# SwiGLU feed-forward: one weight load and ten half-width matmuls change places with a crossbar copy and the gate matmuls behind it

## The chip, the cores and the metric

The kernel runs on one core of a Trainium2 chip. The metric is the device time of one execution in microseconds. Before the change the median of three runs is 163.51 us (163.34 to 163.87).

## What is computed

```python
B, S, D, F = 1, 2048, 640, 1536       # bfloat16, seeded normal values
def reference(x, w_gate, w_up, w_down):
    g = silu(x @ w_gate)              # [2048, 1536]
    u = x @ w_up                      # [2048, 1536]
    return (g * u) @ w_down           # [2048, 640]
```

## The kernel before

The 2048 rows of x are cut into four blocks of 512. D = 640 is five slices of 128 (`KD`), F = 1536 is twelve chunks of 128 (`KF`, "f chunk"). For each block and each f chunk TensorE computes gate (into a PSUM tile `pg`) and up (into `pu`), each as five accumulating matmuls over the slices of D, with the weights stationary and x, turned so that D lies on the partitions (`xT`), streaming through in up to 512 columns. ScalarE then writes `sg`, the Silu of `pg`, to SBUF, and VectorE multiplies it by `pu` into `aT`. After the twelve chunks of a block come the matmuls with `w_down` (`po_t`, `po_a`), their copies out and the stores. Beside all this VectorE computes the last four rows' gate and up as dot products (`do_dots`), from weights that crossbar copies turn (`wgT`, `wuT`).

The change is in `head()`, the first block's first four chunks (`EARLY = 4`), and in the order of the loads ahead of it. x comes in two ways. Rows 0-255 are loaded as they are (`x_sb`), turned on TensorE against an identity, and copied out of PSUM by ScalarE and VectorE. Rows 256-511 are turned on the way in, by a crossbar copy (`turn_x(HALF, S_BLK)`, a `dma_start_transpose`). In the trace this copy is the `DMA_TRANSPOSE` of line 105, the plain weight loads are line 83 (`load_w`) and line 115 (the early gate weights, one slice of D at a time), and every gate or up matmul is line 193 (`proj_step`).

`head()` runs 18 warm-up matmuls on a tile of ones, the turning of rows 0-255, then gate of all four chunks on rows 0-255 (slice by slice, the four chunks in turn, in the order in which the slices of `w_gate` arrive; slice 0 in two pieces of 128 rows), then gate of the four chunks on rows 256-511, and then, chunk by chunk, up on all 512 rows and the Silu and multiply (`gate()`).

```python
        steps = [(0, 0, P), (0, P, HALF)]
        steps += [(kd, 0, HALF) for kd in range(1, KD)]
        steps += [(kd, HALF, S_BLK) for kd in range(KD)]
```

Orders are written out by hand: `keep_order` pins the instructions of TensorE, ScalarE, VectorE and SyncE to the order of the program text. Nearly all loads are issued by SyncE, so its issue order is the order in which they enter its DMA queue: x rows 0-127, four slices of the early gate weights (ScalarE issues x rows 128-255 and one more slice), the crossbar copy of rows 256-511, up of chunks 0-1, up of chunks 2-3, gate and up of chunks 4-7, gate and up of chunks 8-11, `w_down`, the crossbar copy of rows 512-1023, and the inputs of the dot products.

The eight PSUM banks are four for `pg` and `pu` (tag `gu`) and two each under the tags `po_a` and `po_b`; the turning of rows 0-255 and the first four `pu` tiles use the latter four.

Of the kernel before, what the change touches and what calls it, by code (L numbers as in the profile page):

```python
# [10 lines left out]
def _body(  # L11
# [8 lines left out]
    nc = tc.nc  # L20
    P = nc.NUM_PARTITIONS
    f32 = mybir.dt.float32
# [10 lines left out]
    KD = D // P  # L33
    KF = F // P
    S_BLK = 512
    NSB = S // S_BLK
    SUB = S_BLK // P
    HALF = S_BLK // 2
# [4 lines left out]
    WT_STEP = 4  # L43
    ROW_J = 0
    EARLY = 4
    W_CHUNKS = [(4, 8), (8, 12)]
    assert D % P == 0 and F % P == 0 and S % S_BLK == 0 and D > DA and SUB == 4

# [3 lines left out]
    psum = ctx.enter_context(  # L52
        tc.tile_pool(name="psum", bufs=2, space=bass.MemoryType.PSUM)
    )
# [4 lines left out]
    wg_sb = consts.tile([P, KD, F], bf16)  # L59
    wu_sb = consts.tile([P, KD, F], bf16)  # L60
# [15 lines left out]
    wu_v = w_up.rearrange("(kd p) f -> p kd f", p=P)  # L76
    wd_v = w_down.rearrange("(kf p) d -> p kf d", p=P)

    def wslice(a, b):
        return slice(a * P, b * P)  # L80

    def load_w(eng, dst, src, a, b):
        eng.dma_start(out=dst[:, :, wslice(a, b)], in_=src[:, :, wslice(a, b)])
# [14 lines left out]
    def keep_order(engine):  # L98

        traced = [i for i in nc.cur_bb.bb.instructions if i.engine == engine]  # L100
        for a, b in zip(traced, traced[1:]):
            issue_order(a, b)

    def turn_x(r0, r1):
        nc.sync.dma_start_transpose(out=xT[:, :, r0:r1], in_=xt_v[r0:r1])
# [7 lines left out]
    for kd in range(KD):  # L113
        eng = nc.scalar if kd == 1 else nc.sync
        eng.dma_start(
            out=wg_sb[:, kd, wslice(0, EARLY)], in_=wg_v[:, kd, wslice(0, EARLY)]
        )
    turn_x(HALF, S_BLK)
    nc.scalar.activation(silu_first[:], ones[:, 0:1], ACT.Silu)  # L119
    for a in range(0, EARLY, 2):  # L120
        load_w(nc.sync, wu_sb, wu_v, a, a + 2)
    for a, b in W_CHUNKS:
        load_w(nc.sync, wg_sb, wg_v, a, b)
        load_w(nc.sync, wu_sb, wu_v, a, b)
# [49 lines left out]
    def warm(n):  # L174
        for _ in range(n):
            nc.tensor.matmul(  # L176
                pw[:, 0:P], lhsT=ones[:], rhs=ones[:], start=True, stop=True
            )

    def transpose_chunk(c, parts):  # L180
        c_sl = slice(c * P, (c + 1) * P)
        for copy, tag, k0, k1 in parts:
            pt = psum.tile([P, k1 - k0, P], bf16, tag=tag, name="pt")
            for kd in range(k0, k1):
                nc.tensor.transpose(  # L185
                    out=pt[:, kd - k0, :],
                    in_=x_sb[:, c, kd * P : (kd + 1) * P],
                    identity=ident[:],
                )
            copy(out=xT[:, k0:k1, c_sl], in_=pt[:])  # L190

    def proj_step(ps, w_sb, fc, sb, c0, c1, kd):
        nc.tensor.matmul(  # L193
            ps[:, c0:c1],
            lhsT=w_sb[:, kd, fc * P : (fc + 1) * P],
            rhs=xT[:, kd, sb * S_BLK + c0 : sb * S_BLK + c1],
            start=(kd == 0 and c0 in (0, HALF)),
            stop=(kd == KD - 1),
        )

    def proj(ps, w_sb, fc, sb, c0, c1):
        for kd in range(KD):
            proj_step(ps, w_sb, fc, sb, c0, c1, kd)

    def gu_tiles():
        pg = psum.tile([P, S_BLK], f32, tag="gu", name="pg", bufs=4)
        pu = psum.tile([P, S_BLK], f32, tag="gu", name="pu", bufs=4)
        return pg, pu

    def gate(pg, pu, sb, fc, n_s):  # L210

        s0 = sb * S_BLK
        sg = work.tile([P, S_BLK], f32, name="sg")
        nc.scalar.activation(sg[:, 0:n_s], pg[:, 0:n_s], ACT.Silu)  # L214
        nc.vector.tensor_tensor(  # L215
            out=aT[:, fc, s0 : s0 + n_s], in0=sg[:, 0:n_s], in1=pu[:, 0:n_s], op=ALU.mult
        )

    def head():
        dve, act = nc.vector.tensor_copy, nc.scalar.copy  # L220
        split = [(act, "po_a", 0, 2), (dve, "po_b", 2, KD)]
        pgs = [
            psum.tile([P, S_BLK], f32, tag="gu", name="pg", bufs=4)
            for _ in range(EARLY)
        ]
        warm(N_WARM)
        for c in range(HALF // P):
            transpose_chunk(c, split)

        steps = [(0, 0, P), (0, P, HALF)]  # L230
        steps += [(kd, 0, HALF) for kd in range(1, KD)]
        steps += [(kd, HALF, S_BLK) for kd in range(KD)]
        for kd, c0, c1 in steps:
            for fc in range(EARLY):
                proj_step(pgs[fc], wg_sb, fc, 0, c0, c1, kd)

        for fc in range(EARLY):
            pu = psum.tile([P, S_BLK], f32, tag=("po_a", "po_b")[fc % 2], name="pu")
            proj(pu, wu_sb, fc, 0, 0, S_BLK)
            gate(pgs[fc], pu, 0, fc, S_BLK)  # L240
        keep_order(mybir.EngineType.PE)
        keep_order(mybir.EngineType.Activation)

    head()
    for sb in range(NSB):
        n_s = S_BLK if sb < NSB - 1 else S_BLK - T
        for fc in range(KF):
            if sb == 0 and fc < EARLY:
                continue
            pg, pu = gu_tiles()  # L250
# [135 lines left out]
def kernel(tc, *args):  # L386
    _body(tc, *args)
    tc.close()
    tc.compile()
    _trim(tc.nc)  # L390
# [30 lines left out]
```

## Time and profile before

| | before |
|---|---|
| median time | 163.51 us |
| lowest, highest of 3 runs | 163.34, 163.87 us |
| span of the profiled execution, first to last instruction | 161.8 us |
| TensorE busy | 159.4 us (99% of the span) |
| VectorE busy | 111.0 us (69%) |
| ScalarE busy | 42.6 us (26%) |
| HBM read, written | 6.88 MB, 2.62 MB |

The profile was taken in an execution of its own; the page gives its span, and no time with launch and end for it, so that its 161.8 us are set beside the times of the other runs. In the views "PE" is TensorE's matmuls, "PEld" its weight loads, "ACT" ScalarE, "DVE" VectorE, "SPq" and "ACTq" the DMA issues of SyncE and ScalarE. A timeline row gives the start in us, the length from the first of the merged instructions to the end of the last, the engine and line, what is written from what, and the count; the idle time ahead of it and what ended that stand in brackets. A matmul's length includes its passage through the array, so the pace of a stream of matmuls is read from their starts and counts, not from one length. "DMA to landing" is the time from the start of a DMA's issue to the last signal of its data.

### The profile page before, as it was taken

How to read it: one execution, taken by the hardware profiler on the slowest of the kernel's cores; microseconds unless marked ns; L12 is line 12 of the kernel's file. 1: busy time of each engine (PE TensorE's matmuls, PEld its weight loads, DVE VectorE, ACT ScalarE, POOL GpSimd, SP SyncE). 2: the span in 40 equal slices, each digit the busy share in tenths (PEclk: the TensorE clock that was granted, in tenths of full speed). 3: DMA queues.
4: the chain of work that ended last, by engine and by line, in shares of the span. 5: the costliest groups of instructions: out<-in, count | busy, mean ns of one | idle time of the engine just before them, and what ended most of it. 6: DMA issues, size and time to landing. Idle time of an engine off the chain costs nothing.

```text
span 161.8 us, 2142 instructions
## 1 busy us (share of the span) xinstructions
PE 159.4 (99%) x808; PEld 77.6 (48%) x808; DVE 111.0 (69%) x250; ACT 42.6 (26%) x74; POOL 0.6 (0%) x6
## 2 busy tenths in 40 slices
PE   8999999999999999999999999999999999999995
PEld 7854444444444444444444444444444444445454
DVE  2034223599569999989919999979964999993001
ACT  5051222112222222211222322221214222222121
POOL 1000000000000000000000000000000000000000
PEclk9999999999999999999999999999999999999999
DMA  6999999934189999003110000000321000000312
GB/s 212 231 351 349 361 248 231 222 75 91 34 192 159 235 236 184 4 0 34 65 65 0 0 4 2 0 0 3 62 67 34 0 0 0 0 0 4 48 41 73
DMA packets 41961, 15.86 MB, mean 98 GB/s; under 512 B 33504, under 2 KB 41824, under 8 KB 41952
## 3 DMA queue, kind: packets, MB, share of 16 engines
q1 hardware_dynamic: 33584, 14.93, 37.0%
q10 hardware_dynamic: 8368, 0.80, 3.5%
q8 instruction: 6, 0.10, 0.3%
q14 instruction: 3, 0.02, 0.1%
HBM read 6.88 MB, written 2.62 MB: 59 GB/s over the span
## 4 chain that ended last, share of the span: by engine, by line
PE 97%; DMA 2%; SPq 0%; DVE 0%; issue 0%
PE pg L193 32%; PE pu L193 32%; PE po_a L291 26%; PE po_t L261 6%; DMA wg_sb<-in_w_gate_dram 2%; SPq L86 0%; DVE ot_b L302 0%
## 5 line engine op out<-in xcount | busy, mean ns | idle before, releaser
L193 PE MATMUL pg<-xT,wg_sb 128*128 128x512 bf16 (+3 forms) x264 | 59.8, 363 | 0.1
L193 PE MATMUL pu<-xT,wu_sb 128*128 128x512 bf16 (+1 forms) x240 | 59.1, 379 | 0.0
L215 DVE TENSOR_TENSOR aT<-sg,pu 128x512 bf16<-128x512 f32 (+1 forms) x48 | 32.7, 682 | 32.3 <-PE pu L193 32.3
L214 ACT ACTIVATE sg<-pg 128x512 f32<-128x512 f32 (+1 forms) x48 | 28.4, 597 | 71.2 <-PE pg L193 67.4
L291 PE MATMUL po_a<-wd_sb,aT 128*128 128x512 bf16 (+4 forms) x228 | 42.8, 348 | 0.0
L147 DVE SCALAR_TENSOR_TENSOR prod<-wgT,x_row 128x640 f32<-128x640 bf16 x48 | 39.4, 821 | 1.5 <-DMA wgT<-in_w_gate_dram 0.4
L147 DVE SCALAR_TENSOR_TENSOR prod<-wuT,x_row 128x640 f32<-128x640 bf16 x48 | 39.4, 821 | 1.0
L193 PEld LDWEIGHTS <-wg_sb 128*128 128x128 bf16 x264 | 25.9, 100 | 26.8 <-DMA wg_sb<-in_w_gate_dram 0.4
L193 PEld LDWEIGHTS <-wu_sb 128*128 128x128 bf16 x240 | 23.4, 98 | 28.1 <-DMA wu_sb<-in_w_up_dram 0.3
L291 PEld LDWEIGHTS <-aT 128*128 128x128 bf16 x228 | 20.8, 98 | 21.7
L300 ACT CAST ot<-po_a 128x512 bf16<-128x512 f32 (+2 forms) x17 | 9.5, 559 | 31.8 <-PE po_a L291 20.2
L261 PE MATMUL po_t<-aT,wd_sb 128*128 128x512 bf16 (+1 forms) x48 | 10.4, 366 | 0.0
L261 PEld LDWEIGHTS <-wd_sb 128*128 128x128 bf16 x48 | 4.7, 98 | 5.1
L302 DVE CAST ot_b<-po_a 128x96 bf16<-128x96 f32 (+1 forms) x2 | 0.5, 240 | 9.7 <-PE po_a L291 9.6
L270 ACT CAST ot_t<-po_t 128x512 bf16<-128x512 f32 (+1 forms) x4 | 2.2, 559 | 11.6 <-PE po_t L261 11.6
L147 DVE DVE_READ_ACCUMULATOR prod<-wgT,x_row 128x1 f32 x48 | 3.9, 82 | 0.0
L147 DVE DVE_READ_ACCUMULATOR prod<-wuT,x_row 128x1 f32 x48 | 3.9, 82 | 0.0
L272 DVE STREAM_TRANSPOSE ot_q<-ot_t 128x512 bf16<-128x512 bf16 (+1 forms) x4 | 2.7, 676 | 1.7 <-ACT ot_t L270 1.7
L190 DVE COPY xT<-pt 128x384 bf16<-128x384 bf16 x2 | 0.7, 358 | 2.9 <-PE pt L185 2.9
L176 PE MATMUL pw<-ones 128*128 128x128 bf16 x18 | 2.1, 313 | 0.4 <-DVE ones L109 0.4
L176 PEld LDWEIGHTS <-ones 128*128 128x128 bf16 x18 | 1.8, 147 | 0.4 <-DVE ones L109 0.4
L119 ACT ACT_TABLE_LOAD x1 | 1.3, 1283 | 1.0 <-issue 1.0
(13 smaller groups left out, 4.7 us busy)
## 6 DMA issues: line engine op xcount, KB each, us to landing
wd_sb<-in_w_down_dram SPq DMA_DIRECT2D x1, 1920.0 KB, 13.0
out_dram<-ot SPq DMA_DIRECT2D x15, 128.0 KB, 1.7
wg_sb<-in_w_gate_dram SPq DMA_DIRECT2D x2, 640.0 KB, 7.9
wu_sb<-in_w_up_dram SPq DMA_DIRECT2D x2, 640.0 KB, 8.6
wu_sb<-in_w_up_dram SPq DMA_DIRECT2D x2, 320.0 KB, 4.7
x_row<-in_x_dram SPq DMA_DIRECT2D x1, 640.0 KB, 5.1
wg_sb<-in_w_gate_dram SPq DMA_DIRECT2D x4, 128.0 KB, 3.4
out_dram<-ot_q ACTq DMA_DIRECT2D x12, 32.0 KB, 1.9
```

Of the source, the lines that this page charges most:

```text
L119: nc.scalar.activation(silu_first[:], ones[:, 0:1], ACT.Silu)
L147: nc.vector.scalar_tensor_tensor(out=prod[:], in0=wT[:, fc, :], scalar=1.0, in1=x_row[:, t, :], op0=ALU.mult, op1=ALU.mult, accum_out=acc[ ...
L176: nc.tensor.matmul(pw[:, 0:P], lhsT=ones[:], rhs=ones[:], start=True, stop=True)
L190: copy(out=xT[:, k0:k1, c_sl], in_=pt[:])
L193: nc.tensor.matmul(ps[:, c0:c1], lhsT=w_sb[:, kd, fc * P : (fc + 1) * P], rhs=xT[:, kd, sb * S_BLK + c0 : sb * S_BLK + c1], start=(kd == 0 ...
L214: nc.scalar.activation(sg[:, 0:n_s], pg[:, 0:n_s], ACT.Silu)
L215: nc.vector.tensor_tensor(out=aT[:, fc, s0 : s0 + n_s], in0=sg[:, 0:n_s], in1=pu[:, 0:n_s], op=ALU.mult)
L261: nc.tensor.matmul(po_t[:], lhsT=wd_sb[:, kf, DA:D], rhs=aT[:, kf, sb * S_BLK : sb * S_BLK + n_t], start=(kf == 0), stop=(kf == KF - 1),)
L270: nc.scalar.copy(ot_t[:], po_t[:])
L272: nc.vector.transpose(out=ot_q[:], in_=ot_t[:])
L291: nc.tensor.matmul(po[:], lhsT=aT[:, kf, s0 : s0 + P], rhs=wd_sb[:, kf, c0:c1], start=(kf == 0), stop=(kf == KF - 1),)
L300: nc.scalar.copy(ot[:], po[:])
```

## The change

The up weights of chunks 0 and 1 (`UP_FIRST = 2`, 320 KB) are loaded ahead of the crossbar copy of rows 256-511 instead of behind it. On TensorE, up of chunks 0 and 1 on rows 0-255 (ten matmuls of 256 columns) runs between gate on rows 0-255 and gate on rows 256-511. Later, up of these two chunks runs on rows 256-511 alone (ten matmuls of 256 columns), in place of ten matmuls of 512 columns. The four `pu` tiles of `head()` are allocated together ahead of the loops. TensorE has ten matmuls and ten weight loads more in all.

```diff
+    UP_FIRST = 2
...
+    load_w(nc.sync, wu_sb, wu_v, 0, UP_FIRST)
     turn_x(HALF, S_BLK)
     nc.scalar.activation(silu_first[:], ones[:, 0:1], ACT.Silu)
-    for a in range(0, EARLY, 2):
-        load_w(nc.sync, wu_sb, wu_v, a, a + 2)
+    load_w(nc.sync, wu_sb, wu_v, UP_FIRST, EARLY)
...
         steps = [(0, 0, P), (0, P, HALF)]
         steps += [(kd, 0, HALF) for kd in range(1, KD)]
-        steps += [(kd, HALF, S_BLK) for kd in range(KD)]
         for kd, c0, c1 in steps:
             for fc in range(EARLY):
                 proj_step(pgs[fc], wg_sb, fc, 0, c0, c1, kd)
 
+        pus = [
+            psum.tile([P, S_BLK], f32, tag=("po_a", "po_b")[fc % 2], name="pu")
+            for fc in range(EARLY)
+        ]
+        for fc in range(UP_FIRST):
+            proj(pus[fc], wu_sb, fc, 0, 0, HALF)
+        for kd in range(KD):
+            for fc in range(EARLY):
+                proj_step(pgs[fc], wg_sb, fc, 0, HALF, S_BLK, kd)
         for fc in range(EARLY):
-            pu = psum.tile([P, S_BLK], f32, tag=("po_a", "po_b")[fc % 2], name="pu")
-            proj(pu, wu_sb, fc, 0, 0, S_BLK)
-            gate(pgs[fc], pu, 0, fc, S_BLK)
+            proj(pus[fc], wu_sb, fc, 0, HALF if fc < UP_FIRST else 0, S_BLK)
+            gate(pgs[fc], pus[fc], 0, fc, S_BLK)
```

## The prediction

> **What bounds the kernel now.** I read the page first, then the chain of waits in order of time, then the timeline of the first 15 us, and last the single transfers of that stretch.
>
> ```profile
> span 161.8 us, 2142 instructions
> PE 159.4 (99%) x808; PEld 77.6 (48%) x808; DVE 111.0 (69%) x250; ACT 42.6 (26%) x74; POOL 0.6 (0%) x6
> PE 97%; DMA 2%; SPq 0%; DVE 0%; issue 0%
> ```
>
> ```profile
> 0.45 3.21 DMA wg_sb<-in_w_gate_dram
> 3.71 5.21 PE pg L193 x44
> 8.92 4.37 PE pu L193 x20
> 13.29 1.08 PE pg L193 x5
> ...
> 148.85 11.10 PE po_a L291 x84
> ```
>
> TensorE carries 97% of the chain. From 13.29 on every piece of the chain is TensorE's, five matmuls of 512 columns in 1.08 us (0.216 each), one piece behind the other until the last at 148.85. So the span is the time at which TensorE is through its first four chunks, plus a constant. What the change can win or lose lies between 3.71 and about 14, and a microsecond there is a microsecond of the result.
>
> ```profile
> 0.13 0.38 ACTq L86 DMA_DIRECT2D x_sb<-in_x_dram  x1
> 0.45 1.84 SPq L115 DMA_DIRECT2D wg_sb<-in_w_gate_dram  x4
> 2.33 1.91 SPq L105 DMA_TRANSPOSE xT<-in_x_dram  x1
> 4.29 1.15 SPq L83 DMA_DIRECT2D wu_sb<-in_w_up_dram  x2
> 6.06 0.92 SPq L83 DMA_DIRECT2D wu_sb<-in_w_up_dram  x1
> 8.79 4.00 PEld L193 LDWEIGHTS <-wu_sb 128*128 128x128 bf16 x20 [0.15 <-DMA wu_sb<-in_w_up_dram]
> 8.79 4.49 PE L193 MATMUL pu<-xT,wu_sb 128*128 128x512 bf16 x20
> 14.06 0.89 PEld L193 LDWEIGHTS <-wu_sb 128*128 128x128 bf16 x5 [0.19 <-DMA wu_sb<-in_w_up_dram]
> 14.20 1.24 PE L193 MATMUL pu<-xT,wu_sb 128*128 128x512 bf16 x5
> ```
>
> The same timeline, asked for TensorE alone in two narrow windows, shows the place where rows 256-511 are awaited:
>
> ```profile
> 6.27 0.57 PE L193 MATMUL pg<-xT,wg_sb 128*128 128x256 bf16 x3
> 6.57 1.25 PE L193 MATMUL pg<-xT,wg_sb 128*128 128x256 bf16 x10
> ```
>
> And the stretches with their matmul counts (columns: length, TensorE busy and instructions seen, weight loads, granted clock, DMA share, GB/s; instructions that reach in from a neighbouring stretch are counted too):
>
> ```profile
> 0.39:2.30 1.91, 1.91 (x18) 1.83 (x18) 1.00 0.64 187
> 4.96:6.49 1.53, 1.53 (x15) 1.37 (x14) 1.00 0.86 184
> 6.57:8.75 2.18, 2.18 (x21) 1.85 (x19) 1.00 0.97 291
> 8.79:10.96 2.17, 2.17 (x12) 1.00 (x11) 1.00 1.04 349
> ```
>
> The 20 half-width gate matmuls of rows 256-511 take 2.18 us from 6.57 to 8.75, 0.109 each; the ten full-width up matmuls of chunks 0 and 1 take 2.17 us, 0.217 each. The three half-width matmuls of the narrow row begin at 6.27, then one pace on at 6.38, then only at 6.57; the third was due at 6.49. So the wait for the crossbar copy is 0.08 us. The next, for the first up weights, lies between 8.75 and 8.79, 0.04 us. The weight wait at 14.06 costs nothing: the matmul behind it starts at 14.20, which is where 8.79 plus 25 matmuls at 0.216 puts it. **So all the stall that a new order can remove is about 0.12 us, 0.08% of the time.** That is the ceiling of the gain, before any cost.
>
> **When the transfers land.** The tile view of one issue at a time gives issue and landing:
>
> ```profile
> L115 SPq DMA_DIRECT2D wg_sb<-in_w_gate_dram x2: 432/432/432, 1.4 to 1.9; - x2
> DMA to landing us min/median/max: 3.4/3.4/3.4
> L105 SPq DMA_TRANSPOSE xT<-in_x_dram x1: 1914/1914/1914, 2.3 to 2.3; - x1
> DMA to landing us min/median/max: 4.2/4.2/4.2
> L83 SPq DMA_DIRECT2D wu_sb<-in_w_up_dram x1: 583/583/583, 4.3 to 4.3; - x1
> DMA to landing us min/median/max: 4.5/4.5/4.5
> L83 SPq DMA_DIRECT2D wu_sb<-in_w_up_dram x1: 520/520/520, 4.9 to 4.9; - x1
> DMA to landing us min/median/max: 4.9/4.9/4.9
> L83 SPq DMA_DIRECT2D wu_sb<-in_w_up_dram x1: 918/918/918, 6.1 to 6.1; - x1
> DMA to landing us min/median/max: 8.0/8.0/8.0
> ```
>
> The last early gate weights start at 1.86 (the end of the row of four, 2.29, less 0.43) and land at 5.26. The crossbar copy lands at 2.33 + 4.2 = 6.53, and TensorE starts 0.04 later. Up of chunks 0 and 1 lands at 4.29 + 4.5 = 8.79, up of chunks 2 and 3 at 4.93 + 4.9 = 9.83, up of chunks 4 to 7 at 6.06 + 8.0 = 14.06. They land in the order of issue, so I take one transfer's share of the queue as the distance between two landings: 1.04 us for 320 KB of up weights (8.79 to 9.83), 1.27 us for the crossbar copy (5.26 to 6.53).
>
> **The change, part by part.** *SyncE's queue.* The load of chunks 0 and 1 is now issued at 2.33 and the crossbar copy 0.63 later (4.29 to 4.93, the distance of the two up loads), at 2.96. What follows is still issued at 4.93 and later, since the same two instructions stand ahead of it. The copy now shares a completion semaphore with the second x load, which landed at 0.13 + 2.6 = 2.73 by the page:
>
> ```profile
> x_sb<-in_x_dram ACTq DMA_DIRECT2D x1, 160.0 KB, 2.6
> ```
>
> That is before 2.96, so the wait it may add costs nothing.
>
> *Up of chunks 0 and 1 lands earlier.* Behind the gate weights in the queue: 5.26 + 1.04 = 6.30. Bounds: 320 KB at the 349 GB/s of the last stretch above is 0.94 us, 6.20; with the same 4.5 us from issue as before, 2.33 + 4.5 = 6.83. I take 6.30, since the gate weights kept the engines full until then, while before this load met the slump below. TensorE wants it at 6.49, where it used to wait for the copy: no wait. The bounds: none, or 0.34 + 0.04.
>
> *The up matmuls on rows 0-255.* Ten of 0.109, 1.09 us, from 6.49 to 7.58. With their other ten later, 20 half matmuls (2.18) stand for ten full ones (2.17): +0.01.
>
> *The crossbar copy lands later.* 6.30 + 1.27 = 7.57, start of gate on rows 256-511 at 7.61: a wait of 0.03, where the cover ends at 7.58. Bounds: not sooner than 2.96 + 4.2 = 7.16, where TensorE sets the pace; and, if the load's 1.04 comes on top of the later issue, 8.20.
>
> *To the end of the four chunks.* 20 gate matmuls, 2.18, to 9.79; ten up matmuls on the second halves, 1.09, to 10.88. Up of chunk 2 began at 10.96 and now begins at 10.88; its weights, two transfers in the queue as before, landed at 9.83. **The sum is a gain of 0.08 us**, between 0.11 (copy at 7.16) and a loss of 0.55 (copy at 8.20: 8.24 + 3.27 = 11.51).
>
> *ScalarE and VectorE.* The Silu of chunk 0 can't start before its gate is whole, about 9.6 instead of 8.6. The gate accumulators are needed again from chunk 4 on, at 13.1, and four Silus need 2.4 us by
>
> ```profile
> L214 ACT ACTIVATE sg<-pg 128x512 f32<-128x512 f32 (+1 forms) x48 | 28.4, 597 | 71.2 <-PE pg L193 67.4
> ```
>
> so even the last is done near 12 unless the multiply holds it, and VectorE's multiplies follow up as before. Cost nothing, with over 2 us of cover for the first accumulator; without that cover each late Silu would hold TensorE for its 0.6. The four up accumulators taken at once are the banks that the x transposes left before 4 us.
>
> *The load of chunks 4 to 7.* All bytes ahead of it stay ahead of it, so it lands at about 14.06. Its matmul, due at 14.20 - 0.08 = 14.12, still comes behind that. A slip over 0.06 would eat the gain, one for one. What might move it is the slump behind the copy:
>
> ```profile
> 5.25:5.75 0.50, 0.50 (x7) 0.45 (x6) 0.00 (x0) 0.00 (x0) 0.00 (x0) 1.00 1.27 289
> 5.75:6.50 0.75, 0.75 (x9) 0.66 (x7) 0.00 (x0) 0.00 (x0) 0.00 (x0) 1.00 0.51 110
> ```
>
> The queue falls from 289 to 110 GB/s where the crossbar copy hands over to the copies. This goes along with the copy, one slump as before, so I take no slip.
>
> *The clock.* The 18 warm matmuls of 128 columns take 0.106 each, 0.83 ns a column; the half-width ones after 4.96 take 0.109 for 256, 0.43 ns. The array doubles its pace near 4.96, though the granted clock reads 1.00 in both rows. Had it doubled 0.5 us later, about two and a half half-width matmuls would be lost, 0.27 us: TensorE would come to the copy at 6.76, after it landed, and the wait of 0.08 would not be there to remove. The Trainium skill, "TensorE: Matmul & The Clock Gate", Part 1, says that this moment moves by about 500 ns from run to run, since the window that watches activity runs free of the kernel. The trace has one such moment; how it moves, one profile can't show. By this rule the sum would be -0.08 in an execution like this one and +0.01 in one with a late clock.
>
> The profiled execution's span of 161.8 becomes 161.72. The times lie 1.71 above that span (median 163.51), launch and end that the change doesn't touch: 163.43.
>
> **The rivals.** *No effect* (the late clock, or the copy landing near 7.65, where gain and wait cancel): 163.5. For it: the copy misses its time by 0.03 already in my sum, with 0.04 more to break even.
>
> *Slower: the crossbar copy becomes the wait in the gate's way.* Its place is the start of gate on rows 256-511. The copy now stands behind 320 KB more, and only 1.09 us of matmuls were put in its way; from a landing after 7.65 on the kernel loses one for one. At 8.20 it loses 0.55, 164.06; if the up load also keeps its 4.5 us, it lands at 6.83, the copy at 8.10, and the loss is 0.45, 163.96. For it: the cover (1.09) hardly exceeds the load's share (1.04). Against it: the queue ran slack around 6 us (110 GB/s), so that bytes put ahead of the slump may cost less than their own time.
>
> *Faster by more than the stalls of this profile.* Executions with a later copy would have more to win, but the copy's delay passes through the queue to the up load in either order, so the difference stays near 0.1. Only a queue that loses its slump and runs ahead could help, and there is no further stall for it to fill. Against it: the ceiling of 0.12. I leave it a small chance, 162.9, because the three times, 163.34 to 163.87, spread over more than the ceiling.
>
> **How the numbers follow.** A measurement of this kernel can tell about 0.3%, 0.49 us, from no change. Forecast (163.43) 0.38; no effect 0.22; the late copy 0.28, nearly all of its upper part beyond 164.0; faster 0.12. Forecast and no effect fall within 0.3%, as does a little of the late copy: 0.61 within, 0.27 slower, 0.12 faster. The range takes in both bounds of the copy, the spread of the times around them and part of the faster case: 163.0 to 164.2.
>
> **What would show it.** In the changed kernel's profile: the first up matmul on 256 columns near 6.5 without a weight wait over 0.05; ten of these in 1.09; gate on rows 256-511 starting at 7.6; up of chunk 2 at 10.9; the weight load of chunk 4's up still near 14.06. It is wrong if the gate's second half starts after 8.1 or the first up matmul after 6.8 (slower), or if TensorE is anywhere over 0.2 us ahead of today at 13 us (faster).

## The result, and the profile after

The changed kernel takes 163.97 us (median of 21 runs, 163.65 to 164.51), the kernel before, run beside it, 163.63 us (21 runs, 163.19 to 164.07): a ratio of 1.0022, 95% interval 1.0014 to 1.0031. It is slower by about 0.35 us. That is inside the 0.3% named as "no change", and inside the range of 163.0 to 164.2, but it lies on the other side of the forecast, which was a gain of 0.08. Two further comparisons gave 1.0009 (0.9995 to 1.0022) and 1.0021 (1.0007 to 1.0035). The two first profiles show two places: at the gate of chunk 4 the changed kernel is 0.36 us behind, and near 38 us, where the prediction had not looked, it loses 0.44 more. How the loss of the medians divides between the two is not shown; the experiments below come back to it.

The page of the changed kernel, profiled in an execution of 163.95 us:

```profile
span 162.6 us, 2162 instructions
PE 159.5 (98%) x818; PEld 78.0 (48%) x818; DVE 111.0 (68%) x250; ACT 42.5 (26%) x74; POOL 0.6 (0%) x6
```

TensorE's work is the same to 0.1 us; the span has grown by idle time. Its timeline, SyncE and TensorE rows of the first 15 us:

```profile
2.33 0.43 SPq L84 DMA_DIRECT2D wu_sb<-in_w_up_dram  x1
2.91 2.57 SPq L106 DMA_TRANSPOSE xT<-in_x_dram  x1
3.63 1.56 PE L194 MATMUL pg<-xT,wg_sb 128*128 128x128 bf16 x16
5.42 1.05 PE L194 MATMUL pg<-xT,wg_sb 128*128 128x256 bf16 x8 [0.22 <-DMA wg_sb<-in_w_gate_dram]
5.53 0.58 SPq L84 DMA_DIRECT2D wu_sb<-in_w_up_dram  x1
6.74 1.27 PE L194 MATMUL pu<-xT,wu_sb 128*128 128x256 bf16 x10 [0.28 <-DMA wu_sb<-in_w_up_dram]
8.05 2.34 PE L194 MATMUL pg<-xT,wg_sb 128*128 128x256 bf16 x20
10.23 3.41 PE L194 MATMUL pu<-xT,wu_sb 128*128 128x256 bf16 x20
13.48 1.24 PE L194 MATMUL pg<-xT,wg_sb 128*128 128x512 bf16 x5
```

Each step of the forecast can be found here. Up on rows 0-255 begins at 6.74 and not 6.49, with a wait for its weights; gate on rows 256-511 begins at 8.05 and not 7.61; chunk 4's gate begins at 13.48, where it began at 13.12 in the first profile. The bracketed waits count only the time from the end of the matmul before; from pace to pace, the three pauses before 5.42, 6.74 and 8.05 are 0.39, 0.44 and 0.21. The landings, from the tile view of each issue:

```profile
L116 SPq DMA_DIRECT2D wg_sb<-in_w_gate_dram x1: 432/432/432, 1.9 to 1.9; - x1
DMA to landing us min/median/max: 3.9/3.9/3.9
L84 SPq DMA_DIRECT2D wu_sb<-in_w_up_dram x1: 435/435/435, 2.3 to 2.3; - x1
DMA to landing us min/median/max: 4.4/4.4/4.4
L106 SPq DMA_TRANSPOSE xT<-in_x_dram x1: 2569/2569/2569, 2.9 to 2.9; - x1
DMA to landing us min/median/max: 5.1/5.1/5.1
```

The last early gate weights land at 5.75 (forecast 5.26, as before), the up load at 6.7 (forecast 6.30), the copy at 8.0 (forecast 7.57). From gate weights to up load it is 0.94 and from up load to copy 1.32, against 1.04 and 1.27 in the sum. So the shares were right to 0.1, and the starting point was 0.49 off. The stretches of the two kernels, first the changed one, then the one before (columns as in the prediction), show the queue emptier from 3.50 to 4.75, where the sum had it as full as before:

```profile
3.50:4.75 1.25, 1.25 (x17) 1.06 (x16) 0.51 (x2) 0.37 (x1) 0.00 (x0) 1.00 0.69 173
4.75:5.75 1.00, 0.78 (x8) 0.46 (x6) 0.00 (x0) 0.00 (x0) 0.00 (x0) 1.00 1.12 296
```

```profile
3.50:4.75 1.25, 1.10 (x10) 0.99 (x10) 0.36 (x1) 0.15 (x1) 0.00 (x0) 1.00 0.93 266
4.75:5.75 1.00, 1.00 (x10) 0.86 (x9) 0.00 (x0) 0.00 (x0) 0.00 (x0) 1.00 1.16 238
```

The second place is at the first block's output, in the waits and the timeline of the changed kernel:

```profile
ACT ot L308 <- DVE prod L148: 4.2, 1, 4.2
DVE prod L148 <- DMA wgT<-in_w_gate_dram: 0.8, 1, 0.8
PE po_a L299 <- ACT ot L308: 0.3, 1, 0.3
```

```profile
32.52 0.82 DVE L148 SCALAR_TENSOR_TENSOR prod<-wgT,x_row 128x640 f32<-128x640 bf16 x1 [0.82 <-DMA wgT<-in_w_gate_dram]
38.33 1.07 ACT L308 CAST ot<-po_a 128x512 bf16<-128x512 f32 x2 [4.20 <-DVE prod L148]
38.96 0.81 PE L299 MATMUL po_a<-wd_sb,aT 128*128 128x512 bf16 x3 [0.28 <-ACT ot L308]
```

VectorE must do three dot products ahead of the turn of the output (`do_dots(3)`), and they wait for turned gate weights that in this profile land at 32.4 instead of 31.6. ScalarE's stores of the turned output stand behind the turn, its copies of the output tiles behind the stores, and TensorE's third tile needs the bank that the first copy frees: 0.44 us of pause from pace to pace.

The late weights alone do not make this pause. They put the dot products 0.81 later than in the first profile of the kernel before (32.52 against 31.71). That profile had 0.62 us to spare here (below), and TensorE is itself 0.36 later, which makes 0.98. The rest comes from ScalarE's four store issues: one of them takes 1.05 us, where in the kernel before the longest takes 0.50 (durations in ns, least, median, most; changed kernel first):

```profile
L282 ACTq DMA_DIRECT2D out_dram<-ot_q x4: 354/504/1048, 35.8 to 37.8; - x4
```

```profile
L274 ACTq DMA_DIRECT2D out_dram<-ot_q x4: 357/500/501, 34.9 to 36.4; - x4
```

What goes with the long issue is a 16 KB transfer on the queue that loads instructions. In the changed kernel it falls between 35 and 36 us, in the kernel before between 38.5 and 39, behind the stores (packets, MB, share of the DMA engines in the window; changed kernel first):

```profile
q8 instruction: 1, 0.02, 8.5%
```

```profile
q8 instruction: 1, 0.02, 14.4%
```

### The profile page after: what moved, and what is told of

The parts are those of the page before. It is cut to its first block, busy times and chain, and to the rows that moved or that the text cites. A ratio compares the mean times of both kernels' runs of the same rounds, so it can differ in the third digit from the quotient of the medians.

```text
span 162.6 us, 2162 instructions
## 1 busy us (share of the span) xinstructions
PE 159.5 (98%) x818; PEld 78.0 (48%) x818; DVE 111.0 (68%) x250; ACT 42.5 (26%) x74; POOL 0.6 (0%) x6
## 4 chain that ended last, share of the span: by engine, by line
PE 75%; SPq 13%; DMA 7%; DVE 2%; ACTq 1%; issue 1%; ACT 0%; DVEq 0%
PE pu L194 24%; PE pg L194 24%; PE po_a L299 23%; SPq L106 9%; DMA wgT<-in_w_gate_dram 5%; PE po_t L269 4%; SPq L84 2%; DMA x_sb<-in_x_dram 2%; DVE prod L148 2%; ACTq L282 1%; SPq L126 1%; DVE ot_q L280 0%; ACT ot L308 0%; SPq L137 0%; DVE ot_b L310 0%
## 5 line engine op out<-in xcount | busy, mean ns | idle before, releaser
L194 PE MATMUL pu<-xT,wu_sb 128*128 128x512 bf16 (+2 forms) x250 | 59.2, 370 | 0.3 <-DMA wu_sb<-in_w_up_dram 0.3
L194 PEld LDWEIGHTS <-wg_sb 128*128 128x128 bf16 x264 | 25.3, 98 | 27.1 <-DMA wg_sb<-in_w_gate_dram 0.5
L194 PEld LDWEIGHTS <-wu_sb 128*128 128x128 bf16 x250 | 24.4, 98 | 27.6 <-DMA wu_sb<-in_w_up_dram 0.6
L308 ACT CAST ot<-po_a 128x512 bf16<-128x512 f32 (+2 forms) x17 | 9.4, 560 | 32.4 <-PE po_a L299 19.7
```

The costliest lines, as they stand in the source:

```text
L194: nc.tensor.matmul(ps[:, c0:c1], lhsT=w_sb[:, kd, fc * P : (fc + 1) * P], rhs=xT[:, kd, sb * S_BLK + c0 : sb * S_BLK + c1], start=(kd == 0 ...
L308: nc.scalar.copy(ot[:], po[:])
```

## The experiments

**Each half alone.** The theory to begin with: the loss arises among the first four chunks, where the copy lands late (theory 1). Its rival: it arises at the first block's output (theory 2).

```diff
+    load_w(nc.sync, wu_sb, wu_v, 0, 2)     # ahead of turn_x(HALF, S_BLK); head() as before
```

> Only the load of up of chunks 0 and 1 goes ahead of the crossbar copy; TensorE keeps the old order, so gate on rows 256-511 follows gate on rows 0-255 at once and meets the copy uncovered. Both theories read the landings here. By the prediction's queue sum up lands at 6.30 and the copy at 7.57; by the changed kernel's profile at 6.7 and 8.0. Theory 1 (the loss arises among the first four chunks, where the copy lands late): gate's second half starts at 7.6 to 8.0 instead of 6.57, up then meets no wait, chunk 2's up begins 1.0 to 1.4 us later than 10.96, and the time is 0.9 to 1.4 us over before. Theory 2 (the loss arises at the first block's output, where the later transfers reach VectorE's dot products): the same head, and on top a TensorE stall of 0.2 to 0.6 us near 38 us only if the turned gate weights land later than in the kernel before relative to TensorE; as TensorE is later too, that stall should be gone.

Measured 164.68, 1.0067 of before (1.0043 to 1.0091): 1.1 us. TensorE's waits in the timeline of this kernel:

```profile
8.21 2.34 PE L193 MATMUL pg<-xT,wg_sb 128*128 128x256 bf16 x20 [1.69 <-DMA xT<-in_x_dram]
```

The landings are the changed kernel's (5.75, 6.85, 8.17), so they belong to the load order and not to what TensorE does. No pause stands near 38 us, TensorE being later itself.

```diff
     turn_x(HALF, S_BLK)
+    load_w(nc.sync, wu_sb, wu_v, 0, UP_FIRST)   # behind it again; head() as changed
```

> Only TensorE's order is changed; the loads are issued as before, so up on rows 0-255 meets its weights at about 8.8. Both theories: first up matmul at 8.8 instead of 6.5, gate's second half at 9.9, chunk 2's up at 13.15, 2.2 us later than before; the time 1.9 to 2.3 us over before. The matmul order without the load order is worth nothing; it shows whether the 20 half-width matmuls cost more than the 0.01 us of the prediction.

Measured 165.11, 1.0098 (1.0068 to 1.0129), 1.6 us, somewhat less than expected, since in its profile the up load landed at 8.2:

```profile
8.23 1.27 PE L194 MATMUL pu<-xT,wu_sb 128*128 128x256 bf16 x10 [1.80 <-DMA wu_sb<-in_w_up_dram]
9.33 2.35 PE L194 MATMUL pg<-xT,wg_sb 128*128 128x256 bf16 x20
```

Ten half-width up matmuls take 1.10 from start to start, as in the sum, so in TensorE's own time the ten extra matmuls are no cost.

**The dot products out of the way.**

```diff
-        do_dots(3)
+        if sb > 0:
+            do_dots(3)
         nc.vector.transpose(out=ot_q[:], in_=ot_t[:])
+        if sb == 0:
+            do_dots(3)
```

> The kernel before, but in the first block the three dot products that stand ahead of VectorE's turn of the output (and that wait for the turned gate weights) are put behind it. Theory 1: no change, within 0.1%. Theory 2: in executions where the dot products' wait reaches ScalarE's copies and TensorE's third output tile, a stall near 38 us goes; the profile of before had none (0.76 us of slack), but its other executions lie above it, so before gains 0 to 0.3 us.

> The changed kernel with the same move of the three dot products. Theory 1: still 0.2% slower than before, as the changed kernel is. Theory 2: the 0.44 us stall near 38 us is gone, the span falls by 0.3 to 0.5 us, and the kernel stands within 0.1% of the one with the same move of dots on the old order.

On the old order 1.0006 (0.9992 to 1.0019), on the changed one 1.0008 (0.9997 to 1.0019). Beside each other the two stand at 163.55 and 163.56 us (medians of 12), and the pause near 38 us is gone from the second's profile. This looked like theory 2, but the second's chunk 4 still began at 13.50, and both intervals reach far. So both were measured side by side, with further profiles of the kernel before:

> The kernel before once more, unchanged, for a second profile: its first profile, span 161.8, corresponds to one of its fastest times (the other profiles show time minus span of 1.30 to 1.34 us, so about 163.1 where the median is 163.4 to 163.6). Theory 1 (loss among the first four chunks): in an execution of median time the gate of chunk 4 still begins near 13.1, and the missing 0.3 us are elsewhere. Theory 2 (loss at the first block's output): the gate of chunk 4 begins at 13.3 to 13.5 in a median execution too, as in the changed kernel (13.48), and no stall stands near 38 us.

> As the run before it: a third profile of the kernel before. Theory 1: gate of chunk 4 near 13.1. Theory 2: 13.3 to 13.5 at a median time.

> The changed kernel once more, unchanged, timed beside the next one. Both theories: 0.2% over before, median near 163.8 to 164.0. Theory 2: its profile shows a stall of 0.2 to 0.6 us ahead of the third output tile near 38 us again, with the turned gate weights landing after 32.0. Theory 1: gate of chunk 4 at 13.4 or later, and such a stall in this profile or not without the time depending on it.

> The changed kernel with the three dot products behind the turn, once more, in the same call as the changed kernel. Theory 2: 0.25 to 0.45 us under the changed kernel, and within 0.1% of before. Theory 1: the same time as the changed kernel within 0.1%.

The two single executions of the kernel before took 163.97 and 163.40; the changed kernel 163.74, 1.0009 (0.9995 to 1.0022); with the dots moved 163.81, 1.0008 (0.9995 to 1.0022). Side by side, moving the dots won nothing where theory 2 expected 0.25 to 0.45, and the changed kernel's new profile has no pause. Theory 2 as the sole cause is not borne out. Nor did the kernel before begin chunk 4 near 13.1 again, as theory 1 expected: it varies much more than its first profile showed. Chunk 4's gate in its second and third profile:

```profile
13.97 1.24 PE L193 MATMUL pg<-xT,wg_sb 128*128 128x512 bf16 x5
```

```profile
6.90 2.34 PE L193 MATMUL pg<-xT,wg_sb 128*128 128x256 bf16 x20 [0.62 <-DMA xT<-in_x_dram]
13.40 1.24 PE L193 MATMUL pg<-xT,wg_sb 128*128 128x512 bf16 x5
```

In every one of these profiles chunk 4 follows from one landing and the matmuls behind it (microseconds; the landings are those of the slowest of a transfer's signals):

| profile | its time | last early gate weights | up of chunks 0-1 | copy of rows 256-511 | gate of chunk 4 | pause near 38 |
|---|---|---|---|---|---|---|
| before, first | not listed | 5.25 | 8.75 | 6.53 | 13.12 | none |
| before, second | 163.97 | 5.34 | 9.59 | 6.63 | 13.97 | none |
| before, third | 163.40 | 5.54 | 9.01 | 6.86 | 13.40 | none |
| before, dots moved | 162.88 | 4.94 | 8.40 | 6.26 | 12.80 | none |
| changed, first | 163.95 | 5.75 | 6.69 | 8.01 | 13.48 | 0.44 |
| changed, second | 163.40 | 5.59 | 6.58 | 7.89 | 13.37 | none |
| changed, third | 163.68 | 5.58 | 6.56 | 7.88 | 13.36 | 0.33 |
| changed, dots moved | 163.52 | 5.62 | 6.71 | 8.03 | 13.50 | none |
| changed, dots moved, again | 163.83 | 6.06 | 7.02 | 8.36 | 13.83 | none |

In the old order either of two landings can set chunk 4. If it is that of up of chunks 0-1, 20 full-width up matmuls are left: landing plus 4.38 (8.75 and 9.59 give 13.13 and 13.97, the first and second profile). If it is that of the copy, gate's second half comes on top: landing plus 6.54 (6.86 and 6.26 give 13.40 and 12.80, the third profile and the one with the dots moved). In the changed order it is the copy in all five, and gate's second half (2.18), up's two second halves (1.09) and two full chunks (2.16) are left: landing plus 5.47 (8.01, 7.89 and 8.36 give 13.48, 13.36 and 13.83). On average the copy of the new order lands 0.91 sooner than the up load of the old one (8.03 against 8.94) and leaves 1.09 more to do. On the average of these profiles that is a loss of 0.19 us among the first chunks (13.51 against 13.32). With four profiles that spread over 1.17 us and five, the 0.19 is not clear of chance.

There is no third place. From the gate of chunk 4 to the next block's first gate it is 30.22 us in five of these nine profiles, 30.24 and 30.30 in two with the dots moved, and 30.66 and 30.55 in the two with a pause; from there to the end it is 118.47 to 118.49 in all nine.

**Why the gate weights land late.** They stand ahead of everything the change touches.

```diff
+    nc.sync.dma_start(out=wd_sb[:, 0:2, :], in_=wd_v[:, 0:2, :])   # ahead of turn_x(HALF, S_BLK)
```

> The kernel before, with 320 KB of w_down (its first two slices, 256 rows of 1280 bytes) loaded ahead of the crossbar copy, and the rest of w_down where it was. Same bytes in the way as the up load of the change, in 256 pieces instead of 640. It tells why the last early gate weights landed near 5.6 to 6.1 instead of 4.9 to 5.5 when the up load stood behind them. Theory R (the number of pieces: the up load's 640 rows hold up the transfers around them): last gate weights at 5.0 to 5.5 as before, the copy at 7.3 to 7.6. Theory B (the bytes: anything of 320 KB behind the gate weights delays their slowest engines): last gate weights at 5.6 to 6.0, the copy at 7.8 to 8.3. TensorE keeps the old order, so the time is 0.8 to 1.5 us over before in both.

The changed kernel, one chunk instead of two:

```diff
-    UP_FIRST = 2
+    UP_FIRST = 1
...
-    load_w(nc.sync, wu_sb, wu_v, UP_FIRST, EARLY)
+    load_w(nc.sync, wu_sb, wu_v, UP_FIRST, 2)
+    load_w(nc.sync, wu_sb, wu_v, 2, EARLY)
```

> The changed kernel with one chunk instead of two: 160 KB of up ahead of the copy (640 rows of 256 bytes) and five half-width up matmuls ahead of gate on rows 256-511; chunks 1 and 2 to 3 behind the copy. Theory R: last gate weights still near 5.6, chunk 0's up at 6.3 to 6.5, the copy at 7.6 to 7.8, gate of chunk 4 at the copy's landing plus 5.97 (2.22 gate, 0.55 half of chunk 0, 3.24 for three chunks), 13.6 to 13.8. Theory B: last gate weights at 5.4, chunk 0's up at 6.0, the copy at 7.2, gate of chunk 4 at 13.2, about the kernel before.

With the same bytes in 256 pieces (164.49 us, one execution) the landings are those of the changed kernel:

```profile
L115 SPq DMA_DIRECT2D wg_sb<-in_w_gate_dram x1: 432/432/432, 1.9 to 1.9; - x1
DMA to landing us min/median/max: 3.9/3.9/3.9
L118 SPq DMA_DIRECT2D wd_sb<-in_w_down_dram x1: 434/434/434, 2.3 to 2.3; - x1
DMA to landing us min/median/max: 4.3/4.3/4.3
L105 SPq DMA_TRANSPOSE xT<-in_x_dram x1: 2167/2167/2167, 3.0 to 3.0; - x1
DMA to landing us min/median/max: 4.9/4.9/4.9
```

Gate weights at 5.77, copy at 7.92. With half the bytes in 640 pieces they land at 5.36, up at 6.04, the copy at 7.38. So it is not the number of pieces: a plain load of 320 KB behind the gate weights delays their last signals. That more bytes delay them more rests on one profile, whose 5.36 also lies within the range of the old order (4.94 to 5.65), and isn't shown. Why a later entry of the queue slows an earlier one stays open. The kernel with one chunk took 163.66, 1.0013 (1.0000 to 1.0026), not told apart from the changed kernel. Its chunk 4 began at 13.49: its clock came late (below), so that gate's second half began 0.15 behind the copy's landing and not 0.04; the copy alone would have set 13.39. A pause of 0.30 stands near 38 us in its profile.

**Up by slices of D**, an attempt to beat both, with the up loads in their old place:

```diff
-    for a in range(0, EARLY, 2):
-        load_w(nc.sync, wu_sb, wu_v, a, a + 2)
+    for k0, k1 in ((0, 1), (1, 2), (2, 3), (3, 4), (4, KD)):   # or ((0, 2), (2, KD))
+        nc.sync.dma_start(out=wu_sb[:, k0:k1, wslice(0, EARLY)], in_=wu_v[:, k0:k1, wslice(0, EARLY)])
...
+        for kd in range(KD):
+            for fc in range(EARLY):
+                proj_step(pus[fc], wu_sb, fc, 0, 0, S_BLK, kd)
```

> The old place of the up loads (behind the copy), but up of chunks 0 to 3 is loaded by slices of D (five loads of 128 KB, like the early gate weights) and multiplied slice by slice over the four chunks. The theory now held: the time of the first block is the last landing that TensorE waits for plus the matmuls left behind it. In the kernel before the load of up of chunks 0 and 1 lands at 8.4 to 9.6 on its slowest engine and leaves 4.38 us of matmuls; here only 128 KB must be in when gate is through (8.75 to 9.1) and the copy's landing (6.3 to 6.9) plus 6.54 sets the gate of chunk 4: 12.9 to 13.4, against 12.8 to 14.0 before; a gain of 0.1 to 0.4 us. Rival: the slowest engine's delay is shared by every load behind the copy, so the later slices come late instead, and nothing is won.

> As the kernel before it, with two loads (slices 0 and 1, slices 2 to 4) instead of five, so that SyncE issues as many loads as the kernel before. The theory now held: the first, 256 KB, is in by 8.2 to 8.8, gate of chunk 4 at 12.9 to 13.5, a gain of 0.1 to 0.3 us. Rival: none, as above.

Five loads: 163.58, 1.0006 (0.9992 to 1.0021; one of the twelve runs took 166.81). Two loads: 163.36, 0.9992 (0.9979 to 1.0005). Neither is told apart from before. The expected 0.1 to 0.4 did not come. The profiles don't test the theory: in both, TensorE waits for no transfer between the first gate matmul and chunk 4, and a late clock (below) sets its start, 13.54 and 13.75.

**The matmul order without the load**, and the third comparison:

```diff
-            proj(pus[fc], wu_sb, fc, 0, 0, HALF)
+            proj(pus[fc], wg_sb, fc, 0, 0, HALF)   # and the loads in the old order
```

> The changed kernel's matmul order with the loads in the old order. So that the ten up matmuls on rows 0-255 need no load, they take the gate weights of chunks 0 and 1 (up of these two chunks on rows 0-255 is not computed). The theory now held (the loss is the load's: it stands between the gate weights and the copy, and the copy lands about 1.5 us later with only 1.09 us of matmuls put in its way): last gate weights and copy land as before, 5.0 to 5.5 and 6.3 to 6.9, the copy is covered, gate of chunk 4 at 12.8 to 13.3 or later only where the clock is late, and the time is 0.1 to 0.4 us under before. Rival (the matmul order itself costs, through the ten more matmuls or the late Silus): the time stays over before, 0.1 to 0.3 us.

> The changed kernel, timed a third time. The theory now held: 0.1 to 0.3 us over before (the copy's landing, 7.9 to 8.4, plus 5.47, against the up load's, 8.4 to 9.6, plus 4.38), gate of chunk 4 at 13.4 to 13.8. Rival: no difference from before, the first comparison's 0.2% being chance.

The third comparison: 163.78, 1.0021 (1.0007 to 1.0035). The order without the load: 163.64, 1.0006 (0.9990 to 1.0022), no gain where 0.1 to 0.4 was expected. Its gate on rows 256-511 never waits for the copy (6.94), but TensorE then comes to later loads too soon:

```profile
9.82 3.55 PE L194 MATMUL pu<-xT,wu_sb 128*128 128x256 bf16 x20
13.21 1.24 PE L194 MATMUL pg<-xT,wg_sb 128*128 128x512 bf16 x5
14.71 0.60 PE L194 MATMUL pu<-xT,wu_sb 128*128 128x512 bf16 x2 [0.26 <-DMA wu_sb<-in_w_up_dram]
```

Up of chunks 0-1 landed at 9.77, up of chunks 4 to 7 at 14.66. In this profile the stall is handed on from load to load, which shows how taking out one wait can win nothing.

That the matmul order is free, and the loss the load's alone, is not shown. The interval of this kernel reaches from a gain of 0.10% to a loss of 0.22%, so it holds the whole loss.

And the order goes with an effect outside TensorE's own time. In all seven profiles of kernels with the ten extra matmuls (the changed kernel and it with the dots moved, the matmul order alone, the order without the load), the 16 KB instruction load starts at 35.3 to 36.8 us, and one of ScalarE's four store issues takes 0.81 to 1.55 us and ends 0.38 to 0.44 behind the end of that load. In the other nine the load starts at 38.1 to 39.8, behind the stores, and no issue takes over 0.51. So the long issue comes with that load. Why the load comes sooner with the ten extra matmuls is open; with the five extra of the kernel with one chunk it does not (39.8). In both paused profiles of the changed kernel the excess of the issue (0.55 and 0.44) is no less than the pause (0.44 and 0.33), so that the late weights alone would not have made one; in its second profile the weights landed early (31.19), and the long issue alone made none. The pause of the kernel with one chunk came without a long issue, from turned gate weights that landed at 32.86.

## Why the prediction was wrong

**What bounds the kernel** was read rightly as to the place and wrongly as to its steadiness. "The span is the time at which TensorE is through its first four chunks, plus a constant" holds behind the first block: from the next block's first gate to the end it is 118.45 to 118.49 us in all 16 profiles of this study. But the first block is not constant; it holds the pause near 38 us in two of three profiles of the changed kernel and in none of three of the one before. This is one step that failed: the prediction put everything behind 13.29 at nothing, because one chain of waits showed TensorE alone from there; the slack of the chain over the dot products was not looked up, and it cost 0.44, nothing and 0.33. In the timeline of the first profile of the kernel before, ScalarE's first copy of an output tile is this row:

```profile
36.95 0.59 ACT L300 CAST ot<-po_a 128x512 bf16<-128x512 f32 x1 [3.19 <-DMA out_dram<-ot_q]
```

It is done at 37.54, and TensorE comes to its third tile at 38.16: 0.62 us of slack. In the changed kernel's first profile the turned gate weights came 0.8 later and the store issues took 0.55 longer, against TensorE's own 0.36.

**Where the first profile stands** was wrong. The 1.71 us between span and median were taken for launch and end. In every profile with a listed time it is 1.30 to 1.36, so the first profile was an execution of about 163.15, at the fast end of the 21 timed beside the changed kernel (163.19 to 164.07). The stalls it shows, 0.12, were called the ceiling of the gain; the second profile has 0.99 (0.21 at the copy, 0.78 at the up load). More was there to win than the prediction thought, and none was won.

**The step that failed in the sum** is "up of chunks 0 and 1 lands earlier: 5.26 + 1.04 = 6.30". The term is the 5.26: measured 5.58 to 6.06 in the changed kernel and with its dots moved. Up landed at 6.56 to 7.02 and the copy at 7.88 to 8.36, against the sum's 7.57 and a break-even of 7.65. The reason given, "the gate weights kept the engines full until then", does not hold in the changed kernel: 173 GB/s from 3.50 to 4.75. The slump of 110 GB/s, said to "go along with the copy", is no fixed part of the kernel: the same stretch, 5.75 to 6.50, has 214 and 271 GB/s in the second and third profile of the kernel before.

**The rival on the other side was the right one.** The copy became the wait in the gate's way, as it said: the cover (1.09) hardly exceeds the load's share (1.04), and with the gate weights 0.5 late it was not enough. The rival's bound was 8.20, and the copy landed at 8.0. The prediction gave it 0.28, less than the forecast, though the sum lay only 0.08 on the good side of the break-even of 7.65: a margin smaller than the spread of its landings from one execution to the next. Its signs of being wrong (gate's second half after 8.1, the first up matmul after 6.8) were set too wide for that break-even; with 8.05 and 6.74 the changed kernel stays just inside them. That the measured 163.97 meets the rival's 163.96 is luck: the rival's loss was counted on one fast profile, and it knew no pause.

**The parts that held**: the half-width matmuls (1.09 a ten, +0.01), the order of landings, the copy's share (1.31 to 1.34 against 1.27), ScalarE's cover for the accumulators of chunk 4. The shared semaphore did hold the copy's issue (2.91, 0.02 behind the second x load's landing at 2.89), but no later than the sum's 2.96. Up of chunks 4 to 7 moved more than assumed (13.04 in the changed kernel's first profile, 14.02 before), but in the harmless direction.

**The clock** moves as the Trainium skill's page "TensorE: Matmul & The Clock Gate" says in Part 1, but by more than its 500 ns: the pace doubles near 3.5 us in the changed kernel's first profile and near 6.5 in that of up by slices in two loads. In the latter the gate's first half is held by the clock and not by a transfer, as its timeline shows (44 matmuls, the narrow ones first, without a wait):

```profile
3.70 5.90 PE L195 MATMUL pg<-xT,wg_sb 128*128 128x128 bf16 x44
```

Two stretches of the same profile (columns as before):

```profile
4.00:6.40 2.40, 2.40 (x17) 1.90 (x15) 0.30 (x1) 0.00 (x0) 0.00 (x0) 1.00 0.99 221
7.00:8.60 1.60, 1.60 (x17) 1.43 (x16) 0.00 (x0) 0.00 (x0) 0.00 (x0) 1.00 0.94 309
```

17 matmuls, most of them half-width, in 2.40 us, and later as many in 1.60, without a wait between; from start to start a half-width one takes 0.21 up to 6.26 and 0.11 from 6.60 on. In the changed kernel's profiles the clock changes nothing at chunk 4, since the copy sets its start in all of them.

**What stays open**: how much of the loss is the head (0.19 on average here, not clear of chance) and how much the pause near 38 us (0.44, none and 0.33 in three profiles). Moving the dots brought the changed kernel to 1.0008 twice, against 1.0022, 1.0009 and 1.0021 without, and 163.56 against 163.55 for the same move on the old order; but side by side it was 163.81 against 163.74. That both take part is likely, their shares are not shown, nor how much of the pause is the load order's and how much the extra matmuls'.

## What to carry to other kernels

Judge a new order of loads by the last landing that the engine waits for plus the work left behind it, not by the waits that vanish: here, on the average of a few profiles, the last landing came 0.9 us sooner and left 1.1 us more. A load put into a queue can cost those ahead of it as well as those behind it (5.73 against 5.30 here), so the landing of the entry ahead isn't a fixed point. Where one chain of waits shows a single engine, look up the slack of the others behind the change too. And before a ceiling of 0.12 us is read from one profile, find where that execution lies among the timed ones: time minus span of other profiles tells it.

## What the runs showed of the hardware

- A plain load of 320 KB issued behind the early gate weights moved the last of these from 5.30 on average (eight profiles of the old load order, 4.94 to 5.65) to 5.73 (seven with 320 KB behind, 5.58 to 6.06), in 640 pieces or in 256.
- The crossbar copy of rows 256-511 lands 1.28 to 1.34 us behind the plain load ahead of it in all 16 profiles, whether that load landed at 4.94 or at 7.02.
- A DMA issue on ScalarE took 0.81 to 1.55 us instead of 0.50 in the seven profiles in which a 16 KB instruction load overlapped the four store issues, and ended 0.38 to 0.44 us behind its end. In the other nine none took over 0.51.
- The moment at which TensorE's pace doubles lay anywhere from 3.5 to 6.5 us in 16 profiles, with the same 18 warm-up matmuls.
